# A fused causal convolution and softmax-gated MLP: three buffers of output rows instead of two, and the sums of x moved within a step

## The chip, the cores and the metric

The kernel runs on one core of a Trainium2 chip. The metric is device time in microseconds (us) of one execution. A core has five engines that run in parallel and wait for each other by semaphores: PE (TensorE, matrix products; the loading of its stationary operand is listed apart, as PEld), DVE (VectorE), ACT (ScalarE), POOL (GpSimd) and SP (SyncE, which here issues all DMAs). Each engine takes its instructions in the order in which the program lists them. PE writes its products to PSUM, a small memory of banks, from which DVE and ACT read; everything else lies in SBUF.

## The reference

```python
# x: (8, 4160, 192); weight: (8 heads, 7 taps)
w = softmax(weight, axis=-1)
y[b, s, h, :] = sum_k w[h, k] * x_pad[b, s + k, h, :]     # causal, 6 zeros in front
x = y.reshape(33280, 192)
h = x @ w_in                                              # (33280, 1024)
e = exp(h - max(h)); sm = e / (sum(e) + 1e-9)             # by row
solu = h * sm
ln = (solu - mean(solu)) / sqrt(var(solu) + 1e-6) * g_ln
out = ln @ w_out                                          # (33280, 192), float32
```

w_in and w_out arrive as float64; the products are made of float16 halves (a high and a low part).

## The kernel before

**Work.** The 33280 rows are cut into 260 tiles of 128 rows. The convolution works in chunks of half a sequence (2080 rows; sequence 0 is cut into 1024, 1056 and 2080, so that there are 17 chunks, numbered from 0). A chunk belongs to some 16 tiles. A tile goes through: the product with w_in (`emit_rows`, `emit_third`: PE writes `ph`), the scaled maximum (`emit_max`, DVE), the exponential (`emit_exp`, ACT), the product h * e with its sum (`emit_mul`, DVE), the high half (`emit_hi`, ACT: `p`), the sum of squares (`emit_square`, ACT), the low half (`emit_lo`, POOL, then a transposing DMA from `p` to `pT`), and five tiles later the product with w_out (`emit_out`, PE writes `po`) and its removal from PSUM (`emit_evac`, DVE: `raw`).

**Steps.** The order is written out by hand. From tile 8 on `three_steps(i)` issues three tiles a, b, c at a time; all engines' instructions of a step stand in the order of this function. `done` are the three tiles whose second product falls into the step. `place(0)` to `place(3)` are the points at which pieces of the next chunk's convolution are put in.

**Output rows.** Tiles form groups of 8 (the last ones are smaller). A group has one buffer `raw` of 128 x 8 x 192 floats, which the pool hands out under the tag `g_raw` in rotation; `Group.open` takes it at the group's first `emit_evac`. When all eight tiles' sums are there, POOL works out the normalising factors (`Group.roots`), the eight rows are multiplied in place by DVE and POOL in turn (`Group.row`, taken from the list `rows` by `run_rows`), and after every second row a DMA of two tiles is issued (`Group.store`). The pool lets a buffer be taken again only when the four stores of its former group have landed; the waiting instruction is the first evacuation of the new group. The class `Words`, which turns the float64 weights into floats at the start, takes its scratch from the same tag.

**Sums of x.** Each chunk is scaled by a power of two that is found from its size: `sum_squares` makes eight partial values for a chunk of four pieces, for the chunks 0 and 1 by ACT (a square with a sum), for 2 and 3 half by ACT and half by DVE, and later all by DVE (a maximum of absolute values). When the eighth is there (`sum_up`), `square_peaks` (DVE) and a chain of small steps follow: a product with ones on PE (`add_up`), at the next `place`, then some 10 small operations (`run_chain`), and after it the splitting of the chunk's pieces of x into float16 halves (`halve_steps`: ACT or POOL, then two POOL operations a piece; by way of `queue`), which the convolution's products need. `chores` says at which tile of the chunk before which sum is due; `added` deals the sums of a step out to its places `add(0)`, `add(1)` and `add(2)`.

Of the kernel before, what the change touches and what calls it, by code (L numbers as in the profile page):

```python
# [10 lines left out]
I32 = mybir.dt.int32  # L11
# [8 lines left out]
def kernel(  # L20
# [10 lines left out]
    P = 128  # L31
    B, S, D = x.shape
# [15 lines left out]
    GMAX = 8  # L48
# [378 lines left out]
    class Words:  # L427
# [11 lines left out]
        def exponents(self, c):  # L439
            if self.e is None:  # L440
                self.e, self.m = (
                    sp.tile(
                        [P, GMAX * D], I32, name=f"{q}_{self.name}", tag="g_raw", bufs=2
                    )[:, 0 : self.n]
                    for q in "em"
                )
            dve.tensor_scalar(
                self.e[:, c], self.high[:, c], 0x7FF00000, None, ALU.bitwise_and
            )
# [102 lines left out]
    for e, bank in enumerate(banks):  # L552
        for q in range(2 * per):
            j = q // 2
# [314 lines left out]
    class Group:  # L869
# [10 lines left out]
            )  # L880

        def open(self):
            self.raw = self.mk("raw", [P, GMAX, D], 2)

        def roots(self):

# [69 lines left out]
    def chores(ch, k, n):  # L956

        got = {}

        def put(a, z, what, items):  # L960

            for j, item in enumerate(items):
                if int((a + (z - a) * j / len(items)) * n + 1e-9) == k:
                    got.setdefault(what, []).append(item)

        def stage(c, a, m, z, groups):


            put(a, m, "conv", [(c, hg) for hg in groups])
            at = [  # L970
                a + (m - a) * max(j for j, hg in enumerate(groups) if hg[3] <= w)
                / len(groups) for _, w in c.parts
            ]
            put(at[0], 1.0, "open", [c])
            for part, e, f in zip(c.parts, at, [*at[1:], z]):
                turn(c, part, e, f)

        def sums(c, a, z):
            put(a, z, "sum", [(c, h) for j in range(c.np) for h in c.halves(j)])

        def turn(c, part, e, f):
            put(e, f, "turn", [(c, (blk, *part)) for blk in (1, 0, 2)])
            put(e, 1.0, "double", [(c, part)])

        c1, c2, c3 = (chunks[ch + j] if ch + j < NCH else None for j in (1, 2, 3))
        c0 = chunks[ch]
        if ch == 0:
            pass
        elif ch == 1:
            for a, j, z in ((0.0, 0, 2), (0.375, 2, 6), (0.75, 6, 8)):  # L990
                put(a, a + 0.25, "conv", [(c1, hg) for hg in c1.groups()[j:z]])
            put(0.375, 1.0, "open", [c1])
            turn(c1, c1.parts[0], 0.375, 0.38)
        elif c1:
            stage(c1, *((0.25, 0.95, 1.0) if ch == 2 else (0.0625, 0.875, 1.0)), c1.groups())
        if ch == 2:
            turn(c0, c0.parts[1], 0.01, 0.2)
        if c2 and ch < 3:
            sums(c2, *((0.75, 1.0), (0.375, 1.0), (0.0, 0.4))[ch])
        if c3:  # L1000
            if ch:
                put(*((0.0, 0.7) if ch > 2 else (0.25, 0.9 + 0.1 * (ch == 1))), "load",
                    [(c3, j) for j in range(c3.np - (ch == 1))])
                if ch == 2:
                    put(0.0, 1.0, "load", [(c2, c2.np - 1)])
            else:
                put(0.625, 0.875, "load",
                    [(c3, j) for j in range(XR - c1.np - c2.np, c3.np)])
            if ch > 1:
                sums(c3, 0.5, 1.0)  # L1010
        return got
# [82 lines left out]
    def prepare(i):  # L1094
        t = tiles[i]
        c = chunks[t.ch]
        t.yT, t.y2 = c.yT, c.y2
        t.cv = c.cvm if t.k == 0 else c.cv
        pos, n, t.g = t.slot
        if pos not in groups:  # L1100
            groups[pos] = Group(pos, n)
        t.grp = groups[pos]
        return t

    def sum_up(c, h, i):
        c.sum_squares(*h)
        if c.sums == 2 * c.np:
            c.square_peaks()
            follow(c, i)
# [152 lines left out]
    def three_steps(i):  # L1262


        a, b, c = ts = [prepare(i + j) for j in range(3)]
        done = [tiles[j] for j in range(i - DEPTH + (i == PAIRED), i - DEPTH + 3)]
        final = i == NT - 3
        work = others(ts)
        added = work.get("sum", [])
        added = [added[-(-len(added) * j // 3) : -(-len(added) * (j + 1) // 3)] for j in range(3)]  # L1270
        todo = [lambda q=q: (q[0], *conv(*q)) for q in work.get("conv", [])]
        for j in ts:
            if 16 <= j.i < 16 + NQ // 2:
                todo.append(lambda j=j: split_taps((j.i - 16) * 2))
        places = [[], [0], [0, 2], [0, 2, 3], [0, 1, 2, 3]][len(todo)]
        if i == PAIRED:
            places = [2, 3]

        urgent = i == PAIRED + 3
        got = {}  # L1280

        def add(n):
            for c, h in added[n]:
                sum_up(c, h, i + 2)

        def place(n):
            for f in [f for f, m in zip(todo, places) if m == n]:
                got.setdefault(n, []).append(f())
            if n < 2 and chain and chain[0][1] is not None and chain[0][1] <= i + 2:
                if at(n):  # L1290
                    add_up(i + 2, at(n)[0][0].bank)
                elif n:
                    add_up(i + 2)

        def at(n):
            return [q for q in got.get(n, []) if q]

        def uppers(n):
            for k, pc, hg in at(n):
                if not k.scaled and k.exact:  # L1300
                    run_chain(20)
                k.upper(pc, *hg)

        def lowers(n):
            for k, pc, hg in at(n):
                k.lower(pc, *hg)

        def openings():
            for k in work.get("open", []):
                k.open(lefts[k.ch], chunks[k.ch - 1])  # L1310
            for k, piece in work.get("turn", []):
                k.turn(*piece)

        run_stores()
        if final:
            take_rooted()
            emit_a(a, b, c)
            emit_max(a)
        emit_out(done[0])
        place(0)  # L1320
        if not final:

            emit_a(a, b, c, i != 2 * FIRST // P - 2)
        emit_rows(b, False, True)
        emit_evac(done[0])
        place(1)
        uppers(0)
        lowers(0)
        run_chain(4)
        run_rows(i)  # L1330
        for q in squares:
            emit_square(q)
        squares.clear()
        if final:
            ready(tiles[i - 1])
            emit_rows(c, False, True)
        else:
            emit_max(a)
        emit_exp(a)
        uppers(1)  # L1340
        emit_max(b)
        lowers(1)
        emit_exp(b)
        numerators(a)
        emit_lo(a, pool)
        add(0)
        for k, q in doubles:
            k.double(*q)
        doubles.clear()
        if urgent:  # L1350
            openings()
        run_rows(i)
        run_stores()
        for d in done[1:2]:
            emit_out(d)
        place(2)
        for d in done[1:2]:
            emit_evac(d)
        run_chain(4)
        queue.run(3.8 if i < 20 else 2.0)  # L1360
        uppers(2)
        emit_square(a)
        numerators(b)
        emit_lo(b, pool)
        lowers(2)
        add(1)
        if not final:
            emit_rows(c, False, True)
        for d in done[2:]:
            emit_out(d)  # L1370
        place(3)
        emit_max(c)
        emit_exp(c)
        if not at(3):
            emit_square(b)
        run_chain(4)
        for d in done[2:]:
            emit_evac(d)
        uppers(3)
        numerators(c)  # L1380
        lowers(3)
        if at(3):
            emit_square(b)
        add(2)
        if final:
            ready(a)
            ready(b)
        else:
            queue.run(3.8 if i < 20 else 2.0)
        emit_lo(c, dve if final else pool)  # L1390
        squares.append(c)
        run_rows(i)
        if urgent:
            for k, q in work["double"]:
                k.double(*q)
        else:
            openings()
            doubles.extend(work.get("double", []))
        if i == NT - 6:
            ready(b)  # L1400
        queue.run(3.8 if i < 20 else 2.0)
        take_rooted()
# [63 lines left out]
```

## Time and profile before

| | |
|---|---|
| median of 3 runs | 1331.84 us (1331.12 to 1339.61) |
| profiled execution | 1340.51 us, of which its span, first to last instruction, is 1338.6 us |
| busy | PE 1185.7 us (89%), DVE 1019.7 (76%), POOL 961.2 (72%), ACT 945.5 (71%) |
| mean granted clock of PE | 0.957 of full speed |
| output stores (L922) | 127 issues of 192 KB, 2.7 us from issue to landing |

Rows of a profile are read so: line of the program, engine, operation, what is written<-what is read by the names of the program, shape, xcount, then the busy time and the mean ns of one, and behind the second bar the idle time of the engine just before these instructions, with what ended it. In a list of waits, the engine and the line that waited stand left of the arrow, and what released them right of it, with the sum of us, the times and the longest. In a table of windows each stretch has its length and the busy time of each engine in it, with the number of instructions, then the clock granted to PE, the busy share of the DMA engines and what they moved.

### The profile page before, as it was taken

The page shows a single profiled execution, that of the slowest core. Times are in us where ns is not written, and L with a number is a line of the kernel's source. Part 1 is how long each engine was busy: PE and PEld are TensorE (multiplying, and loading weights), DVE is VectorE, ACT ScalarE, POOL GpSimd, SP SyncE. Part 2 cuts the span into 40 slices and gives each one's busy share as a digit, 9 for nine tenths or more (in the row PEclk, how much of TensorE's full clock was granted, in tenths as well). Part 3 has the DMA queues.
Part 4 walks back from the last instruction along what each step waited for, and adds up shares of the span by engine and source line. Part 5 has one row for each costly group of instructions (what it writes and reads, how often), then busy time and mean ns, then how long its engine had stood idle before and what let it go on. Part 6 is the DMA issues. An engine that isn't in the chain of part 4 may idle for free. (4 is left out here: it accounts for less than half of the span.)

```text
span 1338.6 us, 22295 instructions
## 1 busy us (share of the span) xinstructions
PE 1185.7 (89%) x7678; PEld 702.7 (52%) x7678; DVE 1019.7 (76%) x2072; ACT 945.5 (71%) x1541; POOL 961.2 (72%) x949
## 2 busy tenths in 40 slices
PE   6988599999889997998999799799889898998997
PEld 3554355555545554554555455465455554555555
DVE  8777588788768886886877788688677787766775
ACT  7876577677667875776776567677667776866774
POOL 2544587888878686887867678578686966955675
PEclk9899899999989998999999899999889999998998
DMA  8788689999987979989797898969879996988877
GB/s 226 138 172 164 139 160 198 173 167 186 174 192 155 200 154 176 186 167 200 155 199 146 164 192 163 191 121 204 163 153 173 184 162 130 177 153 159 155 156 154
DMA packets 727295, 226.95 MB, mean 170 GB/s; under 512 B 651518, under 2 KB 725774, under 8 KB 727182
## 3 DMA queue, kind: packets, MB, share of 16 engines
q1 hardware_dynamic: 727182, 225.53, 86.1%
q8 instruction: 60, 0.98, 0.3%
q14 instruction: 53, 0.43, 0.1%
HBM read 33.00 MB, written 25.56 MB: 44 GB/s over the span
## 5 line engine op out<-in xcount | busy, mean ns | idle before, releaser
L823 POOL TENSOR_TENSOR p<-e,p 128x1024 f16<-128x1024 f32 x259 | 552.1, 2135 | 288.7 <-ACT p L812 258.6
L839 PE MATMUL po<-ohl,pT 128*128 128x384 f16 (+1 forms) x4200 | 560.2, 291 | 74.8 <-DVE raw L846 49.4
L839 PEld LDWEIGHTS <-pT 128*128 128x128 f16 x4200 | 390.8, 100 | 249.8 <-issue 91.2
L794 ACT ACTIVATE e<-ph,sm 128x1024 f32<-128x1024 f32 x260 | 289.5, 1113 | 227.9 <-DVE ph L787 210.0
L736 PE MATMUL ph<-whi,yT 128*128 128x512 f16 x1548 | 430.3, 388 | 4.9 <-DVE e L804 4.8
L804 DVE SCALAR_TENSOR_TENSOR e<-ph,cv,e 128x1024 f32<-128x1024 f32 x248 | 317.3, 1280 | 68.1 <-ACT e L794 63.1
L812 ACT CAST p<-e 128x1024 f16<-128x1024 f32 x260 | 270.8, 1042 | 132.0 <-DVE e L804 131.5
L787 DVE TENSOR_SCALAR_CACHE_REDUCE ph<-ph,cv 128x1024 f32<-128x1024 f32 x248 | 315.8, 1286 | 41.0 <-PE ph L736 21.4
L736 PEld LDWEIGHTS <-yT 128*128 128x128 f16 x2064 | 197.4, 100 | 236.8 <-issue 48.1
L816 ACT ACTIVATE sq<-e 128x1024 f32<-128x1024 f32 x260 | 273.3, 1051 | 0.1
L846 DVE TENSOR_REDUCE raw<-po 128x192 f32<-128x384 f32 x255 | 140.4, 551 | 114.5 <-DMA out_dram<-raw 51.6
L736 PE MATMUL ph<-wlo,yT 128*128 128x512 f16 x516 | 158.1, 389 | 0.0
L322 DVE SCALAR_TENSOR_TENSOR y<-pc,y 112x432 f16<-112x432 f32 (+5 forms) x140 | 72.3, 533 | 49.7 <-ACT y L313 49.5
L281 PE MATMUL pc<-xs,taps_hi 128*112 128x240 f16 (+1 forms) x448 | 75.8, 267 | 38.7 <-DVE raw L846 26.7
L243 POOL TENSOR_TENSOR xs<-xr,xs 128x960 f16<-128x960 f32 (+1 forms) x56 | 107.5, 1919 | 2.3
L759 PE MATMUL ph<-wlo,yT 64*128 64x512 f16 x269 | 76.2, 385 | 7.9 <-DVE e L804 7.9
L281 PEld LDWEIGHTS <-taps_hi 128*112 128x112 f16 x448 | 51.1, 132 | 41.4 <-issue 26.9
L759 PE MATMUL ph<-wlo,y 64*128 64x512 f16 x251 | 70.4, 383 | 0.0
L181 DVE TENSOR_REDUCE xa<-xr 128x1 f32<-128x384 f32 x112 | 69.1, 620 | 0.0
L313 ACT ACTIVATE y<-pc 112x432 f16<-112x432 f32 (+5 forms) x140 | 62.7, 468 | 8.8 <-PE pc L281 8.0
L240 POOL TENSOR_SCALAR xr<-xr,s 128x960 f32<-128x960 f32 (+1 forms) x56 | 57.5, 1026 | 8.7 <-ACT xs L234 6.4
L281 PE MATMUL pc<-xs,taps_lo 128*112 128x240 f16 (+1 forms) x224 | 59.6, 266 | 0.0
(146 smaller groups left out, 783.7 us busy)
## 6 DMA issues: line engine op xcount, KB each, us to landing
out_dram<-raw SPq DMA_DIRECT2D x127, 192.0 KB, 2.7
xr<-in_x_dram SPq DMA_DIRECT2D x41, 480.0 KB, 4.7
xr<-in_x_dram SPq DMA_DIRECT2D x22, 384.0 KB, 4.0
pT<-p SPq DMA_TRANSPOSE x260, 4.6
y<-yT SPq DMA_DIRECT2D x15, 140.0 KB, 3.1
y<-yT SPq DMA_DIRECT2D x15, 126.0 KB, 3.0
yT<-y SPq DMA_TRANSPOSE x102, 3.7
raw_out<-in_moe_w_out_dram SPq DMA_DIRECT2D x1, 1536.0 KB
```

The source lines that it names most:

```text
L243: (2.1 * size + 0.2, lambda: pool.tensor_tensor(xl, r, h, ALU.subtract)),
L281: nc.tensor.matmul(o, tp[:, h + j, :], r, start=q == 0, stop=q == len(ops) - 1)
L736: nc.tensor.matmul(bank, lhs, w[:, r, n * 512 : (n + 1) * 512], start=start and j == 0, stop=stop and j == len(ops) - 1,)
L759: nc.tensor.matmul(banks_of(t)[n], y[q, t.off : t.off + P], wlo[q, 1, n * 512 : (n + 1) * 512], start=start, stop=not start,)
L787: dve.tensor_scalar(t.ph, t.ph, t.cv[:, 0:1], None, ALU.mult, ALU.min, accum_out=t.bias)
L794: act.activation(t.e, t.ph, AF.Exp, bias=t.bias, scale=-1.0, accum_out=grp.z[:, g : g + 1])
L804: dve.scalar_tensor_tensor(t.e, t.ph, t.cv[:, 3:4], t.e, ALU.mult, ALU.mult, accum_out=t.grp.s1[:, t.g : t.g + 1],)
L812: act.copy(t.p16[:, :, 0, :], t.halves)
L816: act.activation(junk, t.e, AF.Square, accum_out=t.grp.s2[:, t.g : t.g + 1])
L823: eng.tensor_tensor(t.p16[:, :, 1, :], t.halves, t.p16[:, :, 0, :], ALU.subtract)
L839: nc.tensor.matmul(t.po[:, 0:n], t.pT[:, a, :], w, start=j == 0, stop=j == len(ops) - 1)
L846: dve.tensor_reduce(t.grp.raw[:, t.g, :], t.po[:, 0 : 2 * D].rearrange("p (a d) -> p d a", a=2), AX.X, ALU.add,)
```

## The change

Three things are changed. The tag `g_raw` has three buffers instead of two. The sums of chunk 3, which were due from three eighths to the end of chunk 1, are due from its beginning to three quarters. And the sums of a step are dealt out to its first two places in turn, instead of to three places; `add(2)`, which stood behind the last product of the step, is gone.

```diff
@@ Words.exponents
-                        [P, GMAX * D], I32, name=f"{q}_{self.name}", tag="g_raw", bufs=2
+                        [P, GMAX * D], I32, name=f"{q}_{self.name}", tag="g_raw", bufs=3
@@ Group.open
-            self.raw = self.mk("raw", [P, GMAX, D], 2)
+            self.raw = self.mk("raw", [P, GMAX, D], 3)
@@ chores
-            sums(c2, *((0.75, 1.0), (0.375, 1.0), (0.0, 0.4))[ch])
+            sums(c2, *((0.75, 1.0), (0.0, 0.75), (0.0, 0.4))[ch])
@@ three_steps
-        added = [added[-(-len(added) * j // 3) : -(-len(added) * (j + 1) // 3)] for j in range(3)]
+        added = [added[0::2], added[1::2]]
...
-        add(2)
```

What it does to the order is seen on DVE in the step that ends with the last sums of a chunk: tiles 110 to 112, some 600 us into the span. `xa` are the partial values of the chunk, L787 is `emit_max`, L804 `emit_mul`, L846 `emit_evac`, L181 a sum and L217 `square_peaks`. Before:

```order
L804 SCALAR_TENSOR_TENSOR e_6214,s_104_5837<-ph_6182,cv_3715,e_6214 128x1024
L181 TENSOR_REDUCE xa_5913<-xr_2_5671 128x1
L913 TENSOR_SCALAR raw_5722,t_96_5364<-raw_5722,t_96_5365 128x192
L846 TENSOR_REDUCE raw_6147<-po_6232 128x192
L804 SCALAR_TENSOR_TENSOR e_6218,s_104_5837<-ph_6191,cv_3715,e_6218 128x1024
L181 TENSOR_REDUCE xa_5913<-xr_3_5841 128x1
L787 TENSOR_SCALAR ph_6192,sm_6284<-ph_6192,cv_3715 128x1024
L846 TENSOR_REDUCE raw_6147<-po_6267 128x192
L804 SCALAR_TENSOR_TENSOR e_6286,s_112_6161<-ph_6192,cv_3715,e_6286 128x1024
L181 TENSOR_REDUCE xa_5913<-xr_3_5841 128x1
L217 SCALAR_TENSOR_TENSOR xa_5913<-xa_5913 128x8
```

And in the changed kernel:

```order
L804 SCALAR_TENSOR_TENSOR e_6213,s_104_5836<-ph_6181,cv_3714,e_6213 128x1024
L181 TENSOR_REDUCE xa_5912<-xr_2_5670 128x1
L181 TENSOR_REDUCE xa_5912<-xr_3_5840 128x1
L913 TENSOR_SCALAR raw_5721,t_96_5363<-raw_5721,t_96_5364 128x192
L846 TENSOR_REDUCE raw_6147<-po_6232 128x192
L804 SCALAR_TENSOR_TENSOR e_6217,s_104_5836<-ph_6190,cv_3714,e_6217 128x1024
L181 TENSOR_REDUCE xa_5912<-xr_3_5840 128x1
L217 SCALAR_TENSOR_TENSOR xa_5912<-xa_5912 128x8
L787 TENSOR_SCALAR ph_6191,sm_6288<-ph_6191,cv_3714 128x1024
L846 TENSOR_REDUCE raw_6147<-po_6271 128x192
L804 SCALAR_TENSOR_TENSOR e_6290,s_112_6160<-ph_6191,cv_3714,e_6290 128x1024
```

Two sums now stand behind the first product of the step instead of one, and L217 stands ahead of the third tile's maximum, evacuation and product instead of behind them.

The second place is POOL between the low halves (L823) of the tiles 16 and 20. L240 and L243 split chunk 3's pieces of x (`xr`) into halves (`xs`), L909 is a row of the output. Before:

```order
L823 TENSOR_TENSOR p_16_1154<-e_1148,p_16_1154 128x2x512
L909 TENSOR_SCALAR raw_532<-raw_532,t_0_271 128x192
L823 TENSOR_TENSOR p_17_1237<-e_1230,p_17_1237 128x2x512
L208 TENSOR_SCALAR cv_1113<-cv_1113 128x1 x2
L823 TENSOR_TENSOR p_18_1277<-e_1234,p_18_1277 128x2x512
L240 TENSOR_SCALAR xr_0_337<-xr_0_337,s_1112 128x960
L243 TENSOR_TENSOR xs_1319<-xr_0_337,xs_1319 128x960
L240 TENSOR_SCALAR xr_1_341<-xr_1_341,s_1112 128x960
L823 TENSOR_TENSOR p_19_1322<-e_1315,p_19_1322 128x2x512
L909 TENSOR_SCALAR raw_532<-raw_532,t_0_271 128x192
L243 TENSOR_TENSOR xs_1319<-xr_1_341,xs_1319 128x960
```

And in the changed kernel:

```order
L240 TENSOR_SCALAR xr_0_337<-xr_0_337,s_947 128x960
L823 TENSOR_TENSOR p_16_1166<-e_1159,p_16_1166 128x2x512
L243 TENSOR_TENSOR xs_1163<-xr_0_337,xs_1163 128x960
L240 TENSOR_SCALAR xr_1_341<-xr_1_341,s_947 128x960
L909 TENSOR_SCALAR raw_532<-raw_532,t_0_271 128x192
L823 TENSOR_TENSOR p_17_1247<-e_1240,p_17_1247 128x2x512
L243 TENSOR_TENSOR xs_1163<-xr_1_341,xs_1163 128x960
L240 TENSOR_SCALAR xr_2_539<-xr_2_539,s_947 128x960
L823 TENSOR_TENSOR p_18_1286<-e_1244,p_18_1286 128x2x512
L243 TENSOR_TENSOR xs_1163<-xr_2_539,xs_1163 128x960
L240 TENSOR_SCALAR xr_3_642<-xr_3_642,s_947 128x768
L243 TENSOR_TENSOR xs_1163<-xr_3_642,xs_1163 128x768
```

The first two pieces are now split behind the low half of tile 17 at the latest; before, the second piece was split behind that of tile 19.

On ACT, in the step of the tiles 8 to 10 (L812 is `emit_hi`, L313 takes the convolution's product out of PSUM), two squares of chunk 3's pieces (L187) now stand ahead of the first such removal and two behind the second high half; before, all four stood in the step of the tiles 11 to 13. In the changed kernel:

```order
L812 CAST p_8_728<-e_721 128x2x512
L187 ACTIVATE xj_0_734,xa_733<-xr_0_337 128x384
L187 ACTIVATE xj_2_736,xa_733<-xr_1_341 128x384
L313 ACTIVATE y_2_0_776<-pc_0_0_756,s_659 112x5x96
L816 ACTIVATE sq_778,s_8_663<-e_721 128x1024
L812 CAST p_9_781<-e_725 128x2x512
L187 ACTIVATE xj_1_787,xa_733<-xr_0_337 128x576
L187 ACTIVATE xj_3_789,xa_733<-xr_1_341 128x576
```

All four took the place of nothing there; no instruction is added to or taken from any engine, and the DMAs are issued by SP in the same order.

## Prediction

> **What bounds the kernel now.** I read the page's busy times first, then the list of waits over the long middle of the run (227 to 1271 us, where the convolution, both products and the output all run), then the rows around one wait, then tables of windows.
>
> ```profile
> span 1338.6 us, 22295 instructions
> PE 1185.7 (89%) x7678; PEld 702.7 (52%) x7678; DVE 1019.7 (76%) x2072; ACT 945.5 (71%) x1541; POOL 961.2 (72%) x949
> ...
> PE po L839 <- DVE raw L846: 43.0, 15, 7.4
> ...
> PE pc L281 <- DVE raw L846: 25.7, 12, 4.7
> ...
> PE po L839 <- DVE s L112: 15.6, 2, 9.4
> ...
> PEld pc L95 <- DVE xa L217: 6.8, 3, 2.3
> PE ph L759 <- DVE e L804: 6.3, 4, 3.2
> ```
>
> PE is the busiest engine, and where it is idle in the middle of the run it waits for DVE: 43.0 + 25.7 + 15.6 = 84.3 us in 29 waits for an evacuation of output rows or (L112) for a small operation queued right behind one. What DVE itself waits for at L846, from 171 to 1271 us, the view of the tile `raw` says:
>
> ```profile
>   DMA out_dram<-raw: 51.6, 13
>   issue: 33.1, 6
>   POOL p L823: 9.2, 3
>   POOL xr L240: 4.4, 1
> ...
>   PE ph L736: 4.0, 1
>   POOL xs L236: 3.1, 1
> ```
>
> That is 105.4 us in 25 waits, some 40 us apart, once for each group of eight tiles. One of them in order of time, on SP, DVE and PE:
>
> ```profile
> 504.80 2.12 PE L839 MATMUL po<-ohl,pT 128*128 128x384 f16 x16
> 510.95 0.75 SPq L922 DMA_DIRECT2D out_dram<-raw  x1
> 513.73 0.56 DVE L846 TENSOR_REDUCE raw<-po 128x192 f32<-128x384 f32 x1 [7.96 <-DMA out_dram<-raw]
> 514.35 4.00 PE L839 MATMUL po<-ohl,pT 128*128 128x384 f16 x16 [7.42 <-DVE raw L846]
> DMA to landing us min/median/max: 2.1/2.7/5.4
> ```
>
> A store is issued at 510.95 and, with the median landing of 2.7 us, lands at about 513.65; the evacuation that opens a new group starts at 513.73, and PE 0.62 us later. So DVE stands still until the former contents of the one free buffer have left, and everything behind it on DVE stands too. The last row also shows a second price: the 16 products that took 2.12 us before the wait take 4.00 us behind it. The clock says why:
>
> ```profile
> 240.30:243.70 3.40, 3.40 (x11) 0.98 (x11) 1.90 (x8) 2.51 (x4) 2.44 (x2) 0.50 0.82 157
> ...
> 510.00:520.20 10.20, 5.86 (x21) 3.15 (x21) 5.54 (x10) 3.62 (x6) 3.89 (x4) 0.50 0.70 156
> ...
> sum 85.30, PE 61.89 PEld 32.78 DVE 51.40 ACT 35.91 POOL 37.06; mean PE 4.13 PEld 2.19 DVE 3.43 ACT 2.39 POOL 2.47
> 638.80:691.30 52.50, 52.09 (x352) 30.79 (x351) 44.93 (x88) 41.57 (x68) 40.80 (x43) 1.00 0.92 175
> ```
>
> The first three rows are of one table of the middle's 15 windows of half clock, each at a wait of PE: in 85.3 us PE was granted half its clock and was busy for 61.89. The fourth is a stretch of twelve tiles without such a wait: full clock, PE idle for 0.4 us of 52.5.
>
> **The change part by part.** I sum against the profiled execution, 1340.5 us with a span of 1338.6; the median of the runs shown, 1331.84, is 8.7 us below it. I do not correct for that.
>
> *Third buffer.* With three buffers the opening of a group waits for the stores of the group three before instead of two before: about eight tiles, some 40 us, earlier than the landing that ends the wait today. The longest wait in the list above is 8 us, so all 25 go. What is left of PE's waits for L846 I take from the stretch without them: 0.4 us per twelve tiles, so 8 us for the some 240 tiles of the middle. That makes 84.3 - 8 = **76 us**. The half clock goes with them: PE did 61.89 us of work at half speed, which at full speed is 31, so another **31 us**.
>
> *By the Trainium skill*, page "TensorE: Matmul & The Clock Gate", section "Part 1: The HAM clock gate", half clock is the default state that about 3.4 us of activity lifts and an idle window of about 3.4 us brings back, and the penalty is the throttled time times (1 - K/N): half of the 85.3 us, 42.7 us, in place of 31. The trace agrees on the state (0.50 in windows of 3.4 us and its multiples, directly around the waits) but not on the price, as PE was idle in 23.4 of the 85.3 us, and that idle time is in the first term already. By the page the sum below would be 12 us lower.
>
> *Chunk 3's sums three tiles sooner.* The first products of chunk 3's convolution stand in PE's row behind the splitting of its pieces:
>
> ```profile
> 141.01 0.26 PE L281 MATMUL pc<-xs,taps_hi 128*112 128x240 f16 x1 [3.15 <-ACT xs L234]
> 148.77 0.36 PE L281 MATMUL pc<-xs,taps_hi 128*112 128x240 f16 x1 [7.50 <-POOL xs L243]
> 140.07 1.06 POOL L240 TENSOR_SCALAR xr<-xr,s 128x960 f32<-128x960 f32 x1 [3.44 <-ACT xs L234]
> 141.30:151.60 10.30, 2.83 (x10) 1.66 (x10) 1.61 (x5) 2.25 (x4) 8.86 (x7) 0.50 0.43 81
> 126.40:153.10 26.70, 12.55 (x75) 6.89 (x73) 12.44 (x28) 14.39 (x23) 14.64 (x12) 0.81 0.69 122
> ```
>
> PE waits 3.15 + 7.50 us for ACT and POOL, and half of the 2.83 us that follow is lost to the clock: 12 us. In the changed order POOL has the first two pieces behind the low half of tile 17, two tiles before. It has the room: in the 26.7 us of this step (last row, three tiles from one maximum to the next) it is busy for 14.64. What is late next there is POOL itself: four pieces at 1.06 + 2.0 us and four low halves at 2.13 are 21 us, and four tiles last as long once PE's waits are out of the step (26.7 - 10.7 = 16 us for three). But only the first two pieces are needed at once; I count **12 us** gained and, should POOL be late with tile 19, keep 0 as the other end. The ACT side moves four squares (0.60 us each, below) one step up, ahead of an evacuation of the convolution that PE waits for; the step that they leave has the same evacuations behind them. So up to 2.4 us may be lost in the one and won in the other; I take 0.
>
> ```profile
> L187 ACT ACTIVATE xj<-xr 128x384 f32<-128x384 f32 (+1 forms) x16 | 9.6, 602 | 1.7 <-DMA xr<-in_x_dram 1.4
> L181 DVE TENSOR_REDUCE xa<-xr 128x1 f32<-128x384 f32 x112 | 69.1, 620 | 0.0
> 602.63 0.55 DVE L181 TENSOR_REDUCE xa<-xr 128x1 f32<-128x384 f32 x1
> 603.22 0.17 DVE L217 SCALAR_TENSOR_TENSOR xa<-xa 128x8 f32<-128x8 f32 x1
> 603.44 0.39 PE L95 MATMUL pc<-xa,ones 128*128 128x8 f32 x2 [2.05 <-DVE xa L217]
> ```
>
> *Sums in two places.* Where a step's third sum is the last of a chunk, L217 is today behind everything else on DVE, and PE's next `add_up` waits for it: 2.05 us in the row, 6.8 us in the three of the middle. In the new order L217 stands ahead of the third tile's maximum and product (1.29 and 1.28 us) and of an evacuation (0.55), 3.1 us or more sooner, so **6 us** come back. Against it, in some 25 steps the second evacuation and the second tile's product start one sum, 0.62 us, later: 15.5 us if nothing covered it. DVE has the cover in the stretch without waits: 52.5 - 44.93 = 7.6 us idle in four steps, 1.9 us a step. I take 0.
>
> *What is late next.* Without the waits DVE comes close behind PE.
>
> ```profile
> 171.00:1271.00 1100.00, 997.31 (x6506) 587.57 (x6505) 850.58 (x1703) 780.15 (x1256) 836.51 (x816) 0.96 0.88 171
> DVE e L804 <- ACT e L794: 52.7, 60, 0.9
> DVE y L322 <- ACT y L313: 39.7, 49, 1.2
> ```
>
> PE's work at full clock is 997.3 - 31 = 966 us, DVE's with its waits for ACT, which stay, 850.6 + 52.7 + 39.7 = 943. These differ by 23 us in 1100, and DVE's load varies from step to step, so PE will wait in DVE's heavy steps. The cost lies between 0 and those 23 us (if the two simply added their lags); nearest is the stretch of twelve tiles, which says almost nothing, so I take a third, **8 us**, lost.
>
> **Sum:** 76 + 31 + 12 + 6 - 8 = 117 us, and 1340.5 - 117 = 1223.5. I forecast **1223 us**.
>
> **The rivals.** *POOL and the transposes become the bound (1262 us).* `pT` must land before PE uses it.
>
> ```profile
>   DMA pT<-p: 7.8, 6
> DMA to landing us min/median/max: 4.2/4.6/8.0
> L823 POOL TENSOR_TENSOR p<-e,p 128x1024 f16<-128x1024 f32 x259 | 552.1, 2135 | 288.7 <-ACT p L812 258.6
> ```
>
> Today this costs 7.8 us in six waits, though a landing takes up to 8.0 us where 4.6 is the median, and the DMA engines are 88% busy in the middle. Each group puts a burst of small operations and two or three pieces on POOL; the stalls give it time to catch up. If after the change one transposing DMA in each of the 31 groups of eight came late by the 1.3 us that the six average (7.8 / 6), some 39 us would be lost: 1262. Against it: the stretch of twelve tiles above has the DMA engines at 0.92 and no such wait.
>
> *The third buffer frees only half of the waits (1273 us).* The profile names a store in only 13 of 25 waits, 51.6 of 105.4 us; the other 12 might be waits for POOL's rows or something else that a third buffer does not move. Then (76 + 31) x 0.49 + 18 - 3 = 67 us: 1273. Against it: all 25 are at the opening of a group, and rows of POOL stand ahead of the same stores.
>
> *Slower: the half clock comes from load, not from the waits.* If the clock were cut because PE works without pause, it would be cut more. PE has 1185.7 - 31 - 1.4 = 1153 us of work at full clock; with 70 us of idle time left (start, end and the rest, an estimate: 153 us of idle time now, of which 84.3 go), the whole is slower than before once the mean clock falls under 1153 / 1270 = 0.91; at 0.87 it would take 1395. Against it: every half-clock window of the middle lies at a wait, and the stretch of twelve tiles has 1.00 with PE busy all the time.
>
> **How the numbers follow.** My forecast 0.77, POOL and transposes 0.14, half of the waits 0.05, the clock 0.02, nothing measurable 0.02. The forecast's own range: without the 8 us of remaining waits, without the 8 us of lag and with 5 of the 6.3 us of waits for L804 gone 1202; with the 23 us of lag, 15.5 for the sums and no gain at chunk 3 1266. To leave out no more than 2 in 10 the range need only reach the first rival: 1202 to 1264 us. About 1% is what a measurement of this kernel can tell from no change, 13 us here: faster by over that 0.96, within it 0.02, slower 0.02.
>
> **What would show it.** Right: DVE's idle time at L846 falls from over 100 us to under 15 with no store among its causes; PEclk is whole between 170 and 1270 us; PE's waits at L281 for L234 and L243 fall from 11 us to nearly none, and that of L95 for L217 as well; PE's busy time falls by some 32 us although it does the same work; what is left as its idle time are waits of under 2 us for L846, L804 and pT. Wrong: openings that still wait for a store, waits for pT of over 20 us, or half-clock windows without a wait ahead of them.

## Result, and the profile after

The changed kernel takes **1227.53 us** (median of 4 runs, 1226.57 to 1230.61) where the kernel before takes 1331.48 (4 runs, 1329.15 to 1339.61) on the same chip: a ratio of **0.921, 95% interval 0.917 to 0.926**. The profiled execution took 1230.61 us against 1340.5 before, which is 109.9 us less; the medians differ by 104. One execution of one kernel below (chunk 3's sums in one step) took 1330.15 us at a mean granted clock of 0.85, against 1224.67 to 1226.39 in its three others, and is left out of its figures.

The page of the changed kernel first: the span, the busy times, and the groups of the evacuation (L846), of the second product (L839) and of the convolution's product (L281), with the idle time ahead of each behind the last bar.

```profile
span 1228.6 us, 22270 instructions
...
PE 1155.9 (94%) x7678; PEld 685.5 (56%) x7678; DVE 1024.8 (83%) x2072; ACT 946.8 (77%) x1541; POOL 962.1 (78%) x949
...
L839 PE MATMUL po<-ohl,pT 128*128 128x384 f16 (+1 forms) x4200 | 546.2, 286 | 32.9 <-DVE raw L846 17.9
...
L846 DVE TENSOR_REDUCE raw<-po 128x192 f32<-128x384 f32 x255 | 140.2, 550 | 3.0 <-PE po L839 2.9
...
L281 PE MATMUL pc<-xs,taps_hi 128*112 128x240 f16 (+1 forms) x448 | 73.5, 262 | 11.2 <-DVE raw L846 9.7
```

PE does the same 7678 products in 1155.9 us instead of 1185.7, so 29.8 of the 110 us of the span are PE running faster; the other 80.2 are idle time (1338.6 - 1185.7 = 152.9 before, 72.7 now). DVE stands idle ahead of L846 for 3.0 us in all, and only for PE's own product. The view of the tile `raw` from 171 to 1271 us, which began with 51.6 us for stores, has one cause left:

```profile
  PE po L839: 2.3, 6
```

PE's waits in the same window as before (227 to 1271 us, which here reaches past the end at 1228.6), total, times and longest:

```profile
PE po L839 <- DVE raw L846: 9.2, 12, 1.3
PE pc L281 <- DVE raw L846: 8.0, 11, 1.2
PE po L839 <- DVE of L866: 4.9, 2, 3.7
PE po L839 <- DMA pT<-p: 4.0, 7, 2.0
PE ph L759 <- DVE e L804: 3.6, 3, 1.5
...
PE po L839 <- DVE s L112: 1.5, 4, 0.6
```

The 84.3 us for L846 and L112 are 18.7 now, in pieces of 1.3 us at most, and the waits for `xa` (L217) are gone from the list. One opening of a group, in order of time on PE, SP and DVE:

```profile
506.44 2.13 PE L839 MATMUL po<-ohl,pT 128*128 128x384 f16 x16 [0.34 <-DMA pT<-p]
...
508.98 0.63 SPq L922 DMA_DIRECT2D out_dram<-raw  x1
509.53 0.55 DVE L846 TENSOR_REDUCE raw<-po 128x192 f32<-128x384 f32 x1
...
513.33 2.12 PE L839 MATMUL po<-ohl,pT 128*128 128x384 f16 x16
```

The evacuation now starts 0.55 us after the issue of the store that it would have waited for with two buffers, without an idle bracket, and the products behind it take 2.12 us for 16, not 4.00. That store lands at 513.76 us, 4.2 us after the evacuation has started: it no longer matters. The landings that the openings now need lie 24 to 40 us back wherever the trace has them. The clock of the whole middle, in the table of windows (its window too reaches past the end; PEclk is the third number from the end):

```profile
171.00:1271.00 1100.00, 1015.02 (x6843) 602.89 (x6840) 890.99 (x1795) 815.10 (x1307) 871.67 (x859) 1.00 0.93 179
```

0.96 before, 1.00 now, and in the trace no half-clock window stands between 107 and 1216 us; 15 stood between 227 and 1271 us before.

### The profile page after: what moved, and what is told of

Read it like the earlier page. It is cut to its first block, busy times and chain, and to the rows that moved or that the text cites. A ratio compares the mean times of both kernels' runs of the same rounds, so it can differ in the third digit from the quotient of the medians.

```text
span 1228.6 us, 22270 instructions
## 1 busy us (share of the span) xinstructions
PE 1155.9 (94%) x7678; PEld 685.5 (56%) x7678; DVE 1024.8 (83%) x2072; ACT 946.8 (77%) x1541; POOL 962.1 (78%) x949
## 4 chain that ended last, share of the span: by engine, by line
DVE 33%; POOL 21%; issue 16%; PE 12%; ACT 12%; DMA 5%; SPq 2%; ACTq 0%; DVEq 0%; POOLq 0%
POOL p L823 12%; DVE e L804 11%; DVE ph L787 10%; PE ph L736 6%; ACT e L794 5%; PE po L839 4%; ACT p L812 3%; DVE xa L181 3%; DVE y L322 3%; DVE raw L846 2%; DMA pT<-p 2%; ACT y L313 2%; POOL t L903 2%; DVE raw L913 2%; POOL raw L909 1%
## 5 line engine op out<-in xcount | busy, mean ns | idle before, releaser
L823 POOL TENSOR_TENSOR p<-e,p 128x1024 f16<-128x1024 f32 x259 | 552.6, 2137 | 193.0 <-ACT p L812 192.8
L839 PE MATMUL po<-ohl,pT 128*128 128x384 f16 (+1 forms) x4200 | 546.2, 286 | 32.9 <-DVE raw L846 17.9
L839 PEld LDWEIGHTS <-pT 128*128 128x128 f16 x4200 | 381.5, 98 | 204.6 <-issue 38.2
L736 PE MATMUL ph<-whi,yT 128*128 128x512 f16 x1548 | 422.4, 382 | 3.8 <-DVE e L804 3.5
L804 DVE SCALAR_TENSOR_TENSOR e<-ph,cv,e 128x1024 f32<-128x1024 f32 x248 | 317.4, 1280 | 82.4 <-ACT e L794 76.1
L787 DVE TENSOR_SCALAR_CACHE_REDUCE ph<-ph,cv 128x1024 f32<-128x1024 f32 x248 | 315.1, 1286 | 28.1 <-PE ph L736 14.3
L736 PEld LDWEIGHTS <-yT 128*128 128x128 f16 x2064 | 194.3, 99 | 229.5 <-issue 37.3
L812 ACT CAST p<-e 128x1024 f16<-128x1024 f32 x260 | 271.0, 1043 | 60.3 <-DVE e L804 60.0
L736 PE MATMUL ph<-wlo,yT 128*128 128x512 f16 x516 | 154.4, 381 | 0.0
L846 DVE TENSOR_REDUCE raw<-po 128x192 f32<-128x384 f32 x255 | 140.2, 550 | 3.0 <-PE po L839 2.9
L322 DVE SCALAR_TENSOR_TENSOR y<-pc,y 112x432 f16<-112x432 f32 (+5 forms) x140 | 72.3, 533 | 57.9 <-ACT y L313 57.9
L243 POOL TENSOR_TENSOR xs<-xr,xs 128x960 f16<-128x960 f32 (+1 forms) x56 | 107.5, 1921 | 2.3
L281 PE MATMUL pc<-xs,taps_hi 128*112 128x240 f16 (+1 forms) x448 | 73.5, 262 | 11.2 <-DVE raw L846 9.7
L181 DVE TENSOR_REDUCE xa<-xr 128x1 f32<-128x384 f32 (+1 forms) x112 | 66.7, 618 | 0.0
L313 ACT ACTIVATE y<-pc 112x432 f16<-112x432 f32 (+5 forms) x140 | 62.7, 468 | 0.0
L281 PEld LDWEIGHTS <-taps_hi 128*112 128x112 f16 x448 | 49.8, 130 | 21.5 <-DVE raw L846 9.4
L240 POOL TENSOR_SCALAR xr<-xr,s 128x960 f32<-128x960 f32 (+1 forms) x56 | 57.6, 1028 | 2.3
L281 PE MATMUL pc<-xs,taps_lo 128*112 128x240 f16 (+1 forms) x224 | 58.4, 261 | 0.0
```

The source lines that it names most:

```text
L281: nc.tensor.matmul(o, tp[:, h + j, :], r, start=q == 0, stop=q == len(ops) - 1)
L322: dve.scalar_tensor_tensor(self.at(1, col + e, col + z, a, b), pc[:, :, e:z], self.scale(), self.at(0, col + e, col + z, a, b), ALU.mult, ...
L736: nc.tensor.matmul(bank, lhs, w[:, r, n * 512 : (n + 1) * 512], start=start and j == 0, stop=stop and j == len(ops) - 1,)
L787: dve.tensor_scalar(t.ph, t.ph, t.cv[:, 0:1], None, ALU.mult, ALU.min, accum_out=t.bias)
L804: dve.scalar_tensor_tensor(t.e, t.ph, t.cv[:, 3:4], t.e, ALU.mult, ALU.mult, accum_out=t.grp.s1[:, t.g : t.g + 1],)
L812: act.copy(t.p16[:, :, 0, :], t.halves)
```

## Experiments

Twelve kernels ran; each ratio is against runs of the kernel before on the same chip. Between chips the medians of the kernel before lie from 1331.48 to 1337.29 us, so where two kernels ran on different chips the ratios are the better comparison.

### The third buffer alone

The kernel before with

```diff
-                        [P, GMAX * D], I32, name=f"{q}_{self.name}", tag="g_raw", bufs=2
+                        [P, GMAX * D], I32, name=f"{q}_{self.name}", tag="g_raw", bufs=3
...
-            self.raw = self.mk("raw", [P, GMAX, D], 2)
+            self.raw = self.mk("raw", [P, GMAX, D], 3)
```

> The kernel before with the third buffer alone; the sums of x stay where they were. Theory (the wait for the store of the group two before is nearly all of the gain): about 1245 us, that is the changed kernel's 1227.5 plus 8 us of PE waiting for L217 and 11 us of chunk 3's late splitting; DVE's idle time at L846 under 10 us. Rival (the moved sums carry a good part, by freeing the end of each step): 1262 us or more.

Measured: 1238.93 us (1236.2 to 1244.04), ratio 0.929 [0.926, 0.932]. That is 96 us, nine tenths of the changed kernel's gain by the ratios. Of PE's waits after 227 us:

```profile
...
PE pc L95 <- DVE xa L217: 6.2, 3, 2.1
PE pc L281 <- DVE raw L846: 5.6, 10, 0.8
PE po L839 <- DVE raw L846: 4.2, 8, 1.3
```

DVE's idle time at L846 is 2.1 us, PE's waits for L846 are 9.8, and PE is busy for 1158.4 us. The waits at the start for `xs` (8.3 and 3.2 us, 8.1 and 3.1 before) and in the middle for L217 (6.2) stand as before. The first theory holds; its time of 1245 us is 6 too long, as it counted 8 us for the two places of the sums, which two experiments below find to bring nothing.

### The two edits of the sums alone

The changed kernel with `bufs=2` and `2` put back in those two lines.

> The changed kernel with two buffers again; the sums stay moved. Theory: the waits at the opening of a group stay, so 1331.5 minus about 18 us, 1313 us, with over 90 us of DVE idle at L846. Rival (the sums' places matter for the waits too, as rows and stores come sooner without a third sum at the step's end): 1290 us or less.

Measured: 1342.09 us (1338.78 to 1348.26), ratio **1.0046 [1.0019, 1.0074]**: a little slower, which neither theory had. The steps of the tiles 14 and 17 gain as forecast (15.6 and 15.3 us, as in the changed kernel), and then one row takes it all back. The timeline of this kernel:

```profile
153.88 0.46 SPq L922 DMA_DIRECT2D out_dram<-raw  x1
158.78 0.56 DVE L846 TENSOR_REDUCE raw<-po 128x192 f32<-128x384 f32 x1 [11.67 <-issue]
158.90 1.05 SPq L922 DMA_DIRECT2D out_dram<-raw  x2
159.39 0.96 PE L839 MATMUL po<-ohl,pT 128*128 128x384 f16 x3 [11.97 <-DVE raw L846]
```

and the same place in the kernel before:

```profile
153.35 0.47 SPq L922 DMA_DIRECT2D out_dram<-raw  x1
...
158.66 0.56 DVE L846 TENSOR_REDUCE raw<-po 128x192 f32<-128x384 f32 x1
```

In both, the evacuation that opens the third group starts at 158.7 us, 0.2 us after the fourth store of the first group has landed (158.6 here, 158.5 before). Before, PE's waits for `xs` ended at 141.0 and 148.8 us, and the work behind them brought DVE to this evacuation just as the store landed, so the profile showed no wait for a store there. With `xs` sooner DVE is there before the landing and idles for 11.67 us, as the store leaves no sooner (issued at 153.88 us, 153.35 before): PE waits 11.97 us for it instead of 10.65 for `xs`. Two paths met at this evacuation, and shortening one alone bought nothing. In the middle the waits for L846 and L112 rise from 84.3 to 96.5 us, so the 6.1 us that L217 gives up are lost there too.

### Chunk 3's sums back, the rest of the change kept

```diff
-            sums(c2, *((0.75, 1.0), (0.0, 0.75), (0.0, 0.4))[ch])
+            sums(c2, *((0.75, 1.0), (0.375, 1.0), (0.0, 0.4))[ch])
```

> The changed kernel with chunk 3's sums due at the old tiles. Theory: the first 170 us become 11 us longer (the two steps of the tiles 14 to 19 longer by 15, those of 8 to 13 shorter by 4.5), the rest is the same: 1238 us. Rival (POOL's burst moves into a later step and is hidden there): within 3 us of 1227.5.

Measured: 1244.91 us (1242.12 to 1249.18), ratio 0.933 [0.930, 0.936]. So the sooner sums are worth some 16 us on top of the other two edits, not 12 as in the prediction (17 by the medians, 16 by the ratios). And the two places alone, put on the third buffer (first experiment to this one), *cost* 6 us: from the first maximum of tile 14 to that of tile 23 the steps take 69.6 us here and 62.5 there, and PE waits 6.2 us for L846 in these steps instead of 4.9, at a mean granted clock of 0.85 instead of 0.92.

### Output rows scaled and stored sooner, with two buffers

In the kernel before, each of the three places of a step now takes up to two rows of a finished group, where it took one once few were left, so that the fourth store is issued sooner:

```diff
-                for _ in range(4 if i >= NT - 6 else 2 if len(rows) > 4 else 1):
+                for _ in range(4 if i >= NT - 6 else 2):
```

> The kernel before, two buffers, but always two rows of a group at each of the three places of a step instead of one once four are left; so the fourth store leaves about half a step, 6 us, sooner. Theory (each opening waits for the landing of just that store, 4.2 us in the mean): most waits vanish, DVE idle at L846 falls from 105 us to under 35, time about 1250 us. Rival (half of the waits hang on POOL's rows or something else): over 1285 us. Second rival (two rows at once get in DVE's way ahead of the second evacuation): gain under 20 us in spite of vanished waits.

Measured: 1240.95 us (1238.4 to 1241.9), ratio 0.930 [0.927, 0.932]: the whole gain of the third buffer without its memory. What DVE still waits for at L846, whole run:

```profile
  PE po L839: 2.6, 11
  PE ph L736: 2.1, 1
  DMA out_dram<-raw: 1.2, 2
  POOL xs L243: 0.7, 1
```

This settles what the openings waited for. In the kernel before, every opening that waits follows the landing of the fourth store of the group two before by 0.1 to 0.3 us (238.4 to 238.6, 513.6 to 513.7, 630.7 to 630.8 us), whatever name the profile puts on the wait; here the landings come ahead of the openings (first ones: 137.9 for 156.2, 183.0 for 193.2; later ones by 0.1 to 13.6 us) and the waits go. The Trainium skill, page "Perfetto Trace Analysis", section "Optimization Strategy", reads a gap that repeats for a stretch as a possible sign that memory for the next tile has run out. The trace agrees that the buffer was what was missing; these runs add that having it back sooner does as much (1240.95 us) as having one more (1238.93).

### Both: the changed kernel with two buffers and rows sooner

`bufs=2` and `2` as in the second experiment, and the row loop of the one above.

> The changed kernel with two buffers again, and always two rows at each place of a step. Theory (the waits hang on when the fourth store leaves): as the kernel before came to 1241 us by sooner rows and to 1239 by a third buffer, this one comes to about 1230 us. Rival (chunk 3's sooner splitting lets the start catch up with the stores, as with two buffers and moved sums, where an opening at 141 us waited 12 us): some 1238 us, with a wait for a store of over 5 us before 230 us.

Measured: 1230.09 us (1227.88 to 1232.13), ratio 0.921 [0.918, 0.924]: not to be told from the changed kernel. The first group's fourth store lands at 140.2 us and the third group opens at 146.0, so chunk 3's sooner sums are no longer caught by it.

### Three places for the sums, and one sum ahead of the rest, with the rest of the change

Three places as before (`add(2)` put back, and the old thirds):

```diff
-        added = [added[0::2], added[1::2]]
+        added = [added[-(-len(added) * j // 3) : -(-len(added) * (j + 1) // 3)] for j in range(3)]
...
+        add(2)
```

> The changed kernel with the sums in three places again (third buffer and chunk 3's earlier tiles kept). Theory (two sums ahead of the second evacuation cost PE waits for L846, and about as much as is won at L217): PE's waits for L846 in the middle fall by some 7 us, its waits for L217 come back with some 6 us, time 1225 us, within 4 us of the changed kernel. Rival (the two places are worth the 6 us that the prediction gave them): 1234 us.

Measured: 1229.85 us (1227.7 to 1231.97), ratio 0.920 [0.917, 0.923]: the two places are worth nothing that can be measured, as the theory had it. Its waits after 227 us show the exchange: PE's wait for L217 is back with 6.5 us, and those for L846 are 9.4 instead of 17.2.

```profile
PE pc L95 <- DVE xa L217: 6.5, 3, 2.4
...
PE pc L281 <- DVE raw L846: 5.2, 10, 0.8
PE po L839 <- DVE raw L846: 4.2, 8, 1.3
```

With one sum first and the rest behind:

```diff
-        added = [added[0::2], added[1::2]]
+        added = [added[:1], added[1:]]
```

> The changed kernel with the first sum of a step in the first place and all others in the second. Theory: one sum ahead of the second evacuation as before, L217 still ahead of the third tile's maximum, so both gains: PE's waits for L846 fall by some 7 us and those for L217 stay away, time about 1220 us. Rival (a second sum at the second place delays the third tile's maximum and evacuation just as much): within 3 us of the changed kernel.

Measured: 1228.3 us (1226.29 to 1234.98), ratio 0.920 [0.917, 0.922]. The theory's 1220 us is missed and the rival holds: the waits change places again (L846 15.7 us, L804 5.3) and the time doesn't.

### Chunk 3's sums later, in one step

`(0.375, 0.75)` in place of `(0.0, 0.75)`, so that they all stand in the second of its two steps.

> The changed kernel with chunk 3's sums due from three eighths to three quarters of chunk 1, all in the step of the tiles 11 to 13, so that ACT's four squares stand where they stood before. Theory (the squares ahead of the convolution's evacuation cost the step of the tiles 8 to 10 its 2.9 us): that step back to 16.8 us, the next one up by some 2 us as ACT and DVE have all eight sums in it, time about 1226 us. Rival (all in one step is too much for DVE there): 1231 us or more.

Measured: 1224.67 to 1226.39 us, ratio 0.918 [0.914, 0.921]. The rival's 1231 us is ruled out, but the kernel isn't told apart from the changed one, and no trace of it can be set beside the others, so whether the steps of the tiles 8 to 13 lost less is not shown.

### Taking work off DVE

Three ways, on the changed kernel: the maxima over 8 of the 192 columns (which leaves out most of each sum); all rows of the output on POOL; and half of every chunk's sums on ACT.

```diff
-                    self.part[:, col : col + 1], self.raw[j][:, a:z, :], AX.XY,
+                    self.part[:, col : col + 1], self.raw[j][:, a:z, 0:8], AX.XY,
```

> The changed kernel with DVE's maxima taken over 8 of 192 columns of each piece only (the scale is then found from a part of x): DVE loses some 50 us of work. Theory (DVE stands closely behind PE and its lag is what is left): PE's waits for L846, 27 us in the middle and the start, fall under 12 us, time about 1212 us. Rival (POOL and the transposes are next): the waits move to pT, time over 1222 us.

```diff
-                    g.row(j, pool if j % 2 and i < NT else dve)
+                    g.row(j, pool if i < NT else dve)
```

> The changed kernel with all rows of the output multiplied by POOL, none by DVE: DVE loses 128 x 0.49 = 63 us, POOL gains 54 and comes to some 1016 us. Theory (DVE's lag is the cost that is left and POOL has room at 83%): about 1218 us. Rival (POOL and the transposes are the next bound): PE's and PEld's waits for pT rise from 13 to over 30 us and the time to over 1235 us.

```diff
-            self.peaks = 2 * self.np if ch < 2 else self.np if ch < 4 else 0
+            self.peaks = 2 * self.np if ch < 2 else self.np
```

> The changed kernel with half of every later chunk's sums made by ACT (a square with a sum, as for the chunks 2 and 3) instead of DVE: DVE loses some 32 us, ACT gains 41 and comes to 988 us. Theory (DVE's lag is what is left, and the cut sums gave 22 us for 40 us off DVE): about 1215 us. Rival (DVE's waits for ACT, 125 us now, grow by what it saves): within 4 us of 1227.5 or slower.

Measured: 1205.75 us (0.902 [0.898, 0.905]) with the maxima cut, 1221.37 (0.914 [0.911, 0.917]) with the rows on POOL, 1219.88 (0.914 [0.911, 0.917]) with half of the sums on ACT. All three are faster, as each theory had it. DVE's lag, then, is worth some 22 us of what is left by the medians (26 by the ratios, as the chips differ), though DVE is busy for 83% only. What comes up in its place is the transpose. The first three waits of PE after 227 us with the maxima cut, and the first two with the rows on POOL:

```profile
PE po L839 <- DMA pT<-p: 12.6, 14, 1.8
PE po L839 <- DVE of L866: 4.8, 2, 3.7
PE po L839 <- DVE raw L846: 1.5, 3, 0.9
```

```profile
PE po L839 <- DMA pT<-p: 12.3, 13, 2.6
PE pc L281 <- DVE raw L846: 5.5, 7, 1.6
```

Where the changed kernel waits 4.0 us for `pT`, these wait three times as long: it seems that DVE was a little later than POOL and the transposes, and covered them. The two exact versions together:

> The two edits together, all rows on POOL and half of the sums on ACT. Theory: DVE some 95 us lighter; waits for L846 nearly gone, waits for pT as with the rows on POOL alone (12 us): about 1210 us. Rival (what is left after the rows on POOL is POOL and the transposes): no better than 1221 us.

Measured: 1218.44 us (1216.91 to 1221.73), ratio 0.913 [0.909, 0.917], the lowest median of those that compute all, 9 us under the changed kernel (11 by the ratios). It lies between the theory's 1210 us and the rival's 1221, and isn't to be told from either half alone. The reason just given fits but isn't shown: DVE is down to 967.6 us, POOL up to 1010.8, and the waits for `pT` are 13.5 us in the middle.

## Why the prediction was right, point by point

The sum was 117 us against the profiled execution, which lost 109.9; the forecast of 1223 us is 4.5 below the median and 7.6 below the profiled execution after. Some of the nearness to the median is luck: the profiled execution before, from which the sum was taken, lay 9 us above its own median, and the medians differ by 104 us, 13 less than the sum. Term by term, from the two traces:

| step of the prediction | forecast, us | measured, us | from |
|---|---|---|---|
| third buffer: waits for L846 and L112 after 227 us, with the lag of DVE that comes back | -76 + 8 = -68 | -65.6 | 84.3 to 18.7 |
| half clock | -31 | -29.8 | PE's busy time |
| chunk 3's sums | -12 | -10.7 | five steps, tiles 8 to 23 |
| L217 sooner | -6 | -6.1 | 6.1 to 0 |
| the rest | 0 | +2 | what is left of the 110 us |

**Third buffer.** Right, and shown by the first and the fourth experiment: 0 of 25 waits is left, also of the 12 that the profile had not put down to a store. The rival that gave half of them (1273 us) falls with it. The prediction took 8 us as the longest wait where its own list has one of 9.4 (L112); against landings that lie 24 to 40 us back it makes no difference.

**Half clock.** Right in size, and it is a consequence, not a cause: the load rose and the clock rose with it, so the slower rival is gone. Half of PE's work in the throttled time, 31 us, was the right price for the 29.8 that PE's busy time fell by. By the Trainium skill's rule quoted in the prediction ("TensorE: Matmul & The Clock Gate", "Part 1: The HAM clock gate") it would have been 42.7 us; the trace doesn't agree, as the rule also counts throttled time in which PE had nothing to do.

**Chunk 3's sums.** Right for the two `xs` waits (gone; the step of tile 17 falls from 26.7 to 15.3 us) and wrong in a zero. The four squares on ACT and four more sums on DVE were taken as free in the steps they move to. They weren't:

```profile
71.10:90.80 19.70, 13.82 (x74) 7.84 (x71) 11.20 (x23) 14.26 (x29) 10.18 (x14) 0.74 0.83 172
90.80:111.30 20.50, 17.21 (x114) 11.07 (x112) 16.68 (x35) 12.43 (x21) 7.28 (x6) 0.92 0.75 135
...
126.80:142.20 15.40, 14.06 (x92) 7.78 (x91) 11.94 (x25) 14.61 (x27) 15.40 (x11) 1.00 0.55 110
```

The first two rows are the steps of the tiles 8 and 11, which took 16.8 and 18.8 us before: 4.5 us lost. In the first PE waits longer for the convolution's evacuation (3.86 to 5.15 us), in the second for L846 (0.59 to 3.29, while a wait of 2.02 for the convolution's evacuation goes), and the clock falls with it: PE is busy for 31.0 us in the two where it was for 28.3. With chunk 3's sums back (third experiment) they take 36.9 us, so 3.2 of the 4.5 come with these sums; whether the squares on ACT or the sums on DVE do it is not shown. The steps of the tiles 14 and 17 win 14.8. The last row bears out what the prediction named as late next: POOL is busy for all of its 15.4 us, yet PE waits for nothing of it.

The term has no one value, which the prediction did not see: it is nothing with two buffers (second experiment, with the two places), about 11 us with a third buffer and three places (ratios 0.929 to 0.920), some 16 with a third buffer and two places. A term that is added to a sum holds only together with the terms it was added to.

**Sums in two places.** The 6 us were found and given back; this is the step that failed. "I take 0" for a sum ahead of the second evacuation should have been some 8 us: with three places the waits for L846 are 9.4 us, with two 17.2. The prediction's bound of 15.5 had it in range. The idle 1.9 us a step that was to cover it was a mean over steps, and did not cover it.

**What is late next.** Right in kind (waits of at most 1.3 us for L846, scattered) and in size, since 18.7 us are left where 16 were forecast, but the size is partly luck. With three places 10.7 are left (9.4 for L846 and 1.3 for L112), so DVE's lag came out smaller than forecast and some 8 of the 18.7 belong to the sums, which had been put at 0. DVE's waits for ACT did not stay, either: over the whole run those at L804 grew from 63.1 to 76.1 us and those at L322 from 49.5 to 57.9.

**POOL and the transposes.** The rival's price did not come. By the view that the prediction read (7.8 us in six waits before), the waits for `pT` are

```profile
  DMA pT<-p: 16.0, 23
```

That is 8 us more, not 39, and most of the 16.0 stands ahead of PE's weight loads; PE's own waits for `pT` after 227 us are 4.0 us, 1.9 before. It was a right next bound all the same: with DVE lightened they come to 12 to 14 us.

## What to carry to other kernels

Where an engine in order waits for a buffer, price the wait with all that stands behind it and with the clock, and look for the landing that ends it rather than for the name on the wait; freeing the buffer sooner can do what one more buffer does. Before a wait is counted as gained, ask what the same instruction would have waited for next: two paths that reach the same instruction at the same time show as one wait, and shortening either alone buys nothing. An instruction put on the engine that is next behind the bound is not free because that engine is idle on average.

## What the runs showed of the hardware that was not expected

A wait of 2 us can be enough to halve the clock behind it. In the kernel with three places each of the three waits for L217 in the middle is followed by a window of half clock; the first of them in the timeline, and the table of the windows:

```profile
559.39 0.39 PE L95 MATMUL pc<-xa,ones 128*128 128x8 f32 x2 [2.06 <-DVE xa L217]
```

```profile
560.00:563.40 3.40, 3.40 (x12) 1.04 (x11) 1.47 (x6) 1.42 (x3) 3.30 (x3) 0.50 0.99 221
706.80:710.20 3.40, 3.40 (x10) 1.45 (x10) 1.73 (x7) 1.96 (x4) 3.19 (x4) 0.50 1.03 208
925.30:928.70 3.40, 3.40 (x12) 0.78 (x11) 1.95 (x7) 0.54 (x2) 2.94 (x4) 0.51 0.49 93
```

PE is busy for all of the 3.4 us at half clock, so each such wait costs 1.7 us more. In the changed kernel the longest wait for `pT`, 2.0 us, brings none, and its place explains it: within one run all half-clock windows begin on one grid of 3.41 us. Cut along that grid from 200 to 1180 us, the traces of twelve kernels (before, after, and all experiments but the two with the maxima cut and with chunk 3 in one step) have 39 windows at full clock that are followed by one at half clock, and PE was idle for at least 1.89 us in each; in the 3336 that are not, it was idle for at most 1.95. The wait for `pT` lies across an edge of the grid, 1.55 us on one side and 0.44 on the other. So what counts here is some 1.9 us of idle time within one window, in one piece or several. The Trainium skill ("TensorE: Matmul & The Clock Gate", "Part 1: The HAM clock gate") gives an idle window of about 3.4 us as what brings the half clock, and says that the window runs freely. The traces agree on the second and on the length, and put the idle time that it takes at a little over half of one.
